# A shifted-mean LN1 apply, another order of the first loads, and a new step table in a fused adaLN, linear-attention and gated-MLP kernel

## The chip, the cores and the metric

The kernel runs on one core of a Trainium2 chip. The metric is the device time of one execution in microseconds (us); lower is better. The time before is the median of three runs, 279.08 us (278.98 to 279.73). One further execution was profiled; the views of the profile all come from that one.

A core has five engines that run at the same time, each with an in-order queue of its own: PE (TensorE, matmuls; its weight loads are listed as PEld), DVE (VectorE), ACT (ScalarE), POOL (GpSimd) and SP (SyncE, which here only issues transfers). An instruction waits at the head of its queue until the semaphores that it needs have come, and everything behind it on that engine waits with it.

## The reference, cut to what matters

The input is x, 2048 rows of 448 numbers in bf16, and a condition vector c. `mod = silu(c) @ w_mod` gives six vectors of 448: shift, scale and gate for each of two blocks.

```
h = layernorm(x) * (1 + ca) + sa
x = x + ga * A(h)          # attention with softmax feature maps, 16 heads of 28
h = layernorm(x) * (1 + cb) + sb
x = x + gb * B(h)          # gated MLP with a mixing matrix over the rows
```

A takes q, k and v from `h @ wqkv`, maps q and k per head by `w_phi`, and forms the features `concat(softmax(p), softmax(-p))`; `kv` and `z` are sums over all 2048 rows, and the output is `(phi_q kv) / (phi_q z)`, times `wo`. B computes `z = gelu(h @ w_in)`, splits it into z1 and z2 (896 columns each), normalises z2, mixes it over the rows with a 2048x2048 matrix `w_sp`, and returns `(z1 * (w_sp z2 + b_sp)) @ w_out`. Layernorm is `(x - mean) / sqrt(var + eps)` over the 448 columns.

## The kernel before, in words

The rows are cut into 16 tiles of 128. The program is one fixed sequence of some 800 steps. A table, `ORDER`, names them in order; a loop at the end of `fast_path` reads the words one after the other and calls the function of each. A word is `name:arguments/engine@slot`: `l1a:4/G` is step `l1a` for tile 4 on POOL, V is DVE, S is ACT, Y is SP; `@A2` names the PSUM slot. There are five slots, A0, A1 and A2 of two banks and B0 and B1 of one; a step that takes a slot waits until the step that reads out the slot's last user is done. Since the queues are in order, the table fixes each engine's sequence. Nothing is reordered later.

The stages and their steps, in the words of the table:

- **Loads** (`ld:`): x in six pieces (x0 to x5), wq, wk, wv, w_phi, pieces of w_mod (wsa and wca for the first block, wsb and wcb for the second, wmga and wmgb for the gates), wo, w_in in two halves (win0, win1), wout and bsp. They go out on SP's queue (Y) or ACT's (S). `W:t,u` loads a piece of `w_sp` through a transposing transfer, 32 in all, on SP's queue. The transfers of both queues share eight completion semaphores in rotation, so that a transfer is issued only once the eighth transfer before it has landed.
- **Condition**: `ct` and `ce` make silu(c); `csA`, `ccA` (and `csB`, `ccB` for the second block) multiply it with w_mod on PE; `esA`, `ecA`, `esB`, `ecB` read the result out.
- **Weights of the first block**: `FT` transposes wq or wk (raw) on PE, `ET` copies it out, `PF` multiplies it with w_phi, `EP` copies that out into `f_Wq` or `f_Wk`; `SH` adds the shift as a row, `SC` scales the rows by (1 + ca). `SHw` and `SCw` do the same for w_in in the second block.
- **LN1**: `l1s` takes mean and variance of a tile on DVE (L803, L804); `l1e` adds eps (L807); `l1r` raises to the power -0.5 on POOL (L810); `l1a` writes the normalised tile into `f_xpad` (L813), in one instruction of two operations: subtract the mean, multiply with the reciprocal root. Tiles 0 to 3 are then turned on PE (`X`, `XE`), tiles 4 to 15 in pairs by a transposing transfer on SP's queue (`T1:a,b`), into `f_hT`.
- **Features of k and sums**: for each tile `kM` (PE), `kE` and `kF` (two exponentials on ACT), `kS` (sums, DVE), `kR` (reciprocal, DVE), `kP` (multiply, DVE or POOL); `vM` (PE) and `vC` (ACT); `kA` adds the tile's share of kv on PE into slot A0. After the last one `KV` (DVE) reads the sums out. `qM` (PE, eight steps, two per four tiles) with `qE` and `qF` (ACT) make the features of q.
- **Attention output**: `nM` (PE), `nX` (ACT), `nC`, `nS`, `nT` (DVE), `nA`, then a transposing transfer `T2`, `wM` or `wN` (PE; `wN` adds x by an identity matmul), `wR` and `wQ` (sums for LN2).
- **LN2 and w_in**: `l2R`, `l2r`, `l2a` (L973: one instruction that adds the negated mean and multiplies), a transfer `T3`, then `zM` with `zG`, `zQ`, `zR`, `zW`, `zN` for z2 and `yM` with `yG` for z1.
- **Mixing and output**: 28 `gM` of 16 matmuls each, `gG`, then `oM`, `oE` and the store `oD`.

`du` runs matmuls on zeros, which only keep PE running; `tbl` runs one small exponential on ACT. `guard` and `read` take a flag that chooses a general path, which is not taken here.

The lines that the change touches, besides the table, are L807 and L813.

Of the kernel before, what the change touches and what calls it, by code (L numbers as in the profile page):

```python
# [486 lines left out]
l1a:3/G l1s:5 X:2@B1 SCk:3/S PFq:3@A2 SCk:0/V PFq:2@A1 X:3@A0 EPq:3/S XE:2/V PFq:0@B0 SCk:1/S PFq:1@A2 EPq:2/V vM:2@B1 SCk:2/S l1s:6 EPq:1/S kM:0@A1
vC:2 l1s:7 EPq:0/S kM:1@A2 XE:3/V kE:0 l1e:4,8/G kM:2@B0 l1r:4,8 kF:0 l1s:8 kF:1 vM:3@B1 kS:0 kE:2 l1a:6/G SHq@A1 kE:1 l1s:9 kF:2 l1a:5/G kM:3@A2 vC:3
kS:1 SCq:2/S gr:0@B0 SCq:0/S SCq:1/V csB@B1 W:0,7 kF:3 SCq:3/V kR:1 qM:0@A1 ge:0 l1a:4/V esB kE:3 kR:0 l1a:7/V T1:4,6 kP:0/V kP:1/G ccB@B0 kS:2 qF:0
kA:0@A0 T1:6,8 qM:1@A2 kS:3 qE:0 kR:2 ecB kR:3 kP:2/G kA:1@A0 l1s:10 ld:wmgb/Y qF:1 vM:4@B0 l1s:11 W:0,5 qE:1 kM:4@B1 kP:3/G l1s:12 kA:2@A0 vC:4  # L490
l1s:13 kM:5@A2 kE:4 l1s:14 kF:4 kM:6@B0 l1e:8,12/G kE:5 l1r:8,12 kS:4 kA:3@A0 kF:5 kM:7@B1 kE:6 l1a:9/G kS:5 kF:6 qM:2@A2 kE:7 l1a:11/G kR:4 kF:7 kR:5
l1a:8/G kS:6 qM:3@A1 T1:8,10 qE:2 kP:4/V kP:5/G l1s:15 qF:2 kA:4@A0 W:0,6 kR:6 l1a:10/V qE:3 vM:5@B0 vM:6@B1 qF:3 kP:6/V T1:10,12 l1e:12,16/V kM:8@A2
kS:7 l1r:12,16 vC:5 kM:9@A1 ld:wo/S ld:bsp/Y kR:7 kE:8 l1a:12/G l1a:14/V kA:5@A0 kF:8 vM:7@B0 l1a:13/G vC:6 kP:7/V kE:9 vM:8@A2 kF:9 l1a:15/G T1:12,14
kA:6@A0 vC:7 kS:8 kM:10@B1 vC:8 T1:14,16 kA:7@A0 kS:9 wos:2/G kE:10 kM:11@B0 kF:10 kR:8 wos:0/G vM:9@A2 kR:9 kE:11 kS:10 kF:11 vM:10@B1 vC:9 kP:8/V
vM:11@B0 vC:10 kP:9/V kA:8@A0 kR:10 vC:11 kM:12@B1 kS:11 kA:9@A0 kE:12 kP:10/V kM:13@B0 kF:12 kR:11 kA:10@A0 kP:11/G kS:12 kF:13 kM:14@B1 kE:13
vM:12@A2 kR:12 kE:14 kS:13 kP:12/G kF:14 kA:11@A0 vC:12 kM:15@B0 kS:14 ld:win0/S vM:13@B1 kF:15 kR:13 kR:14 kE:15 kA:12@A0 kP:13/V W:0,0 vC:13
vM:14@A2 kP:14/V kA:13@A0 kS:15 vC:14 vM:15@B0 kR:15 kA:14@A0 vC:15 kP:15/G qM:4@A2 ld:win1/S tbl wos:3/G SHw:0@B0 qE:4 kA:15@A0 qM:5@A1 KV:1 qF:4
KV:0 SCw:0,0/S SHw:1@B1 wos:1/V qE:5 nM:0@A2 SCw:1,0/G SCw:2,0/V qF:5 nM:1@A0 SHw:3@B0 nX:1 nX:0 SCw:0,1/S nC:1 nM:2@A1 nC:0 nS:0 SCw:0,3/S SHw:2@B1
# [28 lines left out]
def fast_path(tc, A_x, A_wqkv, A_w_phi, A_wo, B_w_in, B_w_sp, B_b_sp, B_w_out, c, w_mod, out, flag):  # L527
# [277 lines left out]

    def l1e(a, b, eng):
        eng.tensor_scalar(out=rs1[:, a:b], in0=mv1[:, a:b, 1], scalar1=LN_EPS, scalar2=None, op0=ALU.add)  # L807
# [335 lines left out]
```

## Time and profile before

| | us |
|---|---|
| median of three runs | 279.08 |
| lowest, highest | 278.98, 279.73 |
| the profiled execution's own time | 278.33 |
| its span (first to last instruction) | 276.4 |
| PE busy | 258.0 |
| DVE busy | 158.0 |
| ACT busy | 115.1 |
| POOL busy | 79.9 |

The profiled execution took 1.93 us more than its span, and 0.75 us less than the median. In the views, a row of a timeline or of the chain of waits begins with a start and a duration in us; a group's row gives a count, the busy time and the mean duration in ns; a row of the view by windows gives the stretch, its length, the busy time of each engine with its number of instructions, the clock that PE was granted (1.00 is full), the busy share of the DMA engines, and GB/s.

### The profile page before, as it was taken

The numbers are of one execution on the slowest core, as the hardware profiler recorded it, in microseconds if no ns is written. First come the engines' busy times: TensorE is split into PE (matmuls) and PEld (weight loads), VectorE is DVE, ScalarE is ACT, GpSimd is POOL, SyncE is SP. The second block draws the span as 40 slices with busy tenths as digits, with TensorE's granted clock in tenths as the row PEclk, the third lists the DMA queues.
The fourth block names the chain that finished last, engine by engine and source line by source line (L and its number), as shares of the span: only waits on it lengthen the run. The fifth ranks groups of instructions, "written<-read, shape, count | busy, mean of one in ns | idle before, by whom it ended". The sixth has DMA issues, their size and how long they took to land.

```text
span 276.4 us, 4119 instructions
## 1 busy us (share of the span) xinstructions
PE 258.0 (93%) x1522; PEld 133.4 (48%) x1533; DVE 158.0 (57%) x371; ACT 115.1 (42%) x242; POOL 79.9 (29%) x86
## 2 busy tenths in 40 slices
...
GB/s 187 285 289 61 87 88 162 168 35 192 43 76 107 161 147 115 51 193 103 137 185 162 21 0 0 2 0 17 50 92 166 48 2 53 16 0 33 2 35 76
DMA packets 68654, 25.21 MB, mean 91 GB/s; under 512 B 58129, under 2 KB 68498, under 8 KB 68626
## 3 DMA queue, kind: packets, MB, share of 16 engines
...
## 4 chain that ended last, share of the span: by engine, by line
PE 76%; POOL 6%; DVE 6%; issue 4%; ACT 3%; DMA 3%; POOLq 0%; DVEq 0%; ACTq 0%
PE g_ps L1025 35%; PE z_ps L984 9%; PE z_ps L1012 9%; PE o_ps L1037 7%; POOL f_xpad L813 4%; PE v_ps L844 3%; PE k_ps L836 3%; PE x_ps L944 3%; PE q_ps L884 3%; PE kvacc L867 2%; DMA f_hT<-f_xpad 1%; DVE f_t L928 1%; DMA f_x<-in_A_x_dram 1%; ACT f_win L757 1%; ACT f_Eq L889 1%
## 5 line engine op out<-in xcount | busy, mean ns | idle before, releaser
L1025 PEld LDWEIGHTS <-f_z2n 128*128 128x128 bf16 x448 | 43.7, 98 | 52.4
L1030 DVE TENSOR_TENSOR f_gb<-g_ps,f_bsp 128x512 f32<-128x512 f32 x28 | 19.3, 690 | 57.6 <-PE g_ps L1025 57.5
L1025 PE MATMUL g_ps<-f_Eq,f_z2n 128*128 128x512 bf16 x218 | 49.2, 379 | 0.3
L1015 ACT ACTIVATE f_z1T<-z_ps 128x512 bf16<-128x512 f32 x28 | 15.7, 598 | 53.8 <-PE z_ps L1012 53.7
L984 PE MATMUL z_ps<-f_win,f_hT 112*128 112x448 bf16 (+1 forms) x128 | 26.0, 352 | 0.1
L1012 PE MATMUL z_ps<-f_hT,f_win 113*128 113x512 bf16 (+1 forms) x112 | 25.8, 379 | 0.0
L1025 PE MATMUL g_ps<-f_hT,f_z2n 128*128 128x512 bf16 x110 | 24.6, 379 | 0.1
L1025 PE MATMUL g_ps<-f_wsp,f_z2n 128*128 128x512 bf16 x109 | 24.0, 379 | 0.2
L813 POOL TENSOR_SCALAR f_xpad<-f_x,f_mv,f_rs 128x448 bf16<-128x448 bf16 x12 | 22.8, 1909 | 0.5
L1037 PE MATMUL o_ps<-f_wout,f_z1T 128*128 128x448 bf16 x112 | 22.3, 353 | 0.0
L850 DVE TENSOR_REDUCE f_ksum<-f_E 128x32 f32<-128x896 bf16 x16 | 16.9, 1067 | 7.0 <-ACT f_E L839 7.0
L1031 DVE TENSOR_TENSOR f_z1T<-f_gb,f_z1T 128x512 bf16<-128x512 f32 x28 | 19.5, 696 | 1.2
L839 ACT ACTIVATE f_E<-k_ps 128x448 bf16<-128x448 f32 x32 | 15.6, 551 | 6.8 <-issue 4.2
L984 PEld LDWEIGHTS <-f_hT 112*128 112x128 bf16 (+1 forms) x128 | 12.4, 97 | 12.2 <-issue 0.3
L836 PE MATMUL k_ps<-f_Wk,f_hT 113*128 113x448 bf16 (+1 forms) x64 | 14.3, 355 | 3.8 <-DMA f_hT<-f_xpad 3.8
L889 ACT ACTIVATE f_Eq<-q_ps 112x1024 bf16<-112x1024 f32 x16 | 15.6, 1024 | 4.7 <-PE q_ps L884 4.7
L1012 PEld LDWEIGHTS <-f_win 113*128 113x128 bf16 (+1 forms) x112 | 10.8, 97 | 12.6
L928 DVE TENSOR_TENSOR f_t<-num,f_w 128x896 bf16<-128x896 f32 x16 | 16.8, 1083 | 0.2
L1037 PEld LDWEIGHTS <-f_z1T 128*128 128x128 bf16 x112 | 10.9, 98 | 10.6
L988 ACT ACTIVATE f_z2g<-z_ps 128x896 bf16<-128x896 f32 x16 | 14.7, 916 | 2.0 <-PE z_ps L984 1.9
L844 PE MATMUL v_ps<-f_wv,f_hT 113*128 113x448 bf16 (+1 forms) x64 | 15.3, 379 | 0.0
L857 POOL TENSOR_TENSOR f_phik<-f_E,f_kr 128x896 bf16<-128x896 bf16 x7 | 11.8, 1687 | 12.3 <-DVE f_kr L854 8.7
...
## 6 DMA issues: line engine op xcount, KB each, us to landing
...
f_wmg<-in_w_mod_dram SPq DMA_DIRECT2D x2, 392.0 KB, 6.6
...
```

The lines of the kernel that those rows point to most:

```text
L813: eng.tensor_scalar(out=xpad[:, i % NX, :, 0:CB], in0=x_sb[:, i, :].rearrange("p (k e) -> p k e", k=KC), scalar1=mv1[:, i, 0:1], scalar2=r ...
L836: nc.tensor.matmul(t[:, 0, 0:D], lhsT=hT[0:KR[m], i, m, :], rhs=Wk[0:KR[m], m, :], start=(m == 0), stop=(m == KC - 1))
L844: nc.tensor.matmul(t[:, 0, 0:D], lhsT=hT[0:KR[m], i, m, :], rhs=wv[0:KR[m], m, :], start=(m == 0), stop=(m == KC - 1))
L850: nc.vector.tensor_reduce(out=ksum[:, i], in_=Er[i % NR][:].rearrange("p s (c f h) -> p (s c) h f", c=4, h=HP), axis=AX.X, op=ALU.add)
L889: nc.scalar.activation(out=Eq[st // 2][0:CB, 2 * c2:2 * c2 + 2, s, (st % 2) * 512:(st % 2 + 1) * 512], in_=ps["q" + str(n)][0:CB, :, :], f ...
L928: nc.vector.tensor_tensor(out=tr[i % 2][:], in0=numv(i)[:, :, :, 0:DH], in1=wr[i // 2 % 2][:, i % 2].unsqueeze(3).to_broadcast([P, 2, H, D ...
L984: nc.tensor.matmul(t[:, hf, 0:D], lhsT=hT[0:KR[m], i, m, :], rhs=win_s[0:KR[m], m, FH + hf * D:FH + (hf + 1) * D], start=(m == 0), stop=(m ...
L1012: nc.tensor.matmul(t[:, 0, :], lhsT=win_s[0:KR[m], m, fc * P:(fc + 1) * P], rhs=hT[0:KR[m], 4 * st:4 * st + 4, m, :], start=(m == 0), stop ...
L1025: nc.tensor.matmul(g[:, 0, :], lhsT=later["z2n"][:, s_, fc * P:(fc + 1) * P], rhs=wspT[t][:, s_, :], start=(s_ == 0), stop=(s_ == NT - 1))
L1030: nc.vector.tensor_tensor(out=gb[:], in0=ps["G%d_%d" % (t, fc)][:, 0, :], in1=bsp[:, t * TCHF:(t + 1) * TCHF], op=ALU.add)
L1031: nc.vector.tensor_tensor(out=z, in0=gb[:], in1=z, op=ALU.mult)
L1037: nc.tensor.matmul(ps["o" + str(t)][:, 0, 0:D], lhsT=later["z1T"][:, fc, t * P:(t + 1) * P], rhs=wout_s[:, fc, :], start=(fc == 0), stop=( ...
```

## The change

Three things change. `l1e` gets a second instruction, which writes the negated mean of the same tiles into a new array `f_nm`, and `l1a` adds that instead of subtracting the mean; the multiplication stays. The first loads go out in another order: c is first on ACT's queue with wq behind it, and x0 is first on SP's, followed by w_phi and wk. The table is new as a whole: the same steps (but for the `du` words, which now run 19 matmuls instead of 27), many in other places, on other slots and some on other engines. On other engines are, counted over the table: `SCw` 10 on ACT (before 7, with 2 on POOL and 1 on DVE), `SCv` 4 on ACT (3), `ET` all four on ACT (2 of 4), `l2a` 8 on POOL (4 of 16), `wR` 11 on ACT (9), `wQ` 10 on ACT (13), `zN` 3 on POOL (6), `nA` 6 on POOL (4), `XE` 3 on ACT (1), and one step each of `EP`, `zQ` and two of `wos`; 11 of the 16 tiles of the attention output go by `wN` (9). `kP` and `l1a` keep their split between DVE and POOL.

```
 ORDER = """
-ld:x0/S ld:wsa/Y ld:x1/Y ld:c/Y m1/V m2b/G du:15@A2 ld:wv/Y ld:wca/Y m3 l1s:0 ld:wk/Y m2a/G ld:x2/Y l1e:0,1/V ld:phi/Y m4 ld:wq/Y l1s:1 ct@B0 ld:x3/Y
...
+ld:c/S ld:x0/Y ld:wq/S ld:phi/Y tbl ld:wk/Y m3 du:1@A2 m1/V ld:x1/Y m2b/G ct@B0 ld:wsa/Y du:8@A2 ce:1 l1s:0 ld:x2/Y m4 ld:wca/Y ce:2 ld:wv/Y m2a/G
+FTq:0@B1 ld:x3/Y ce:3 bd/V W:0,1 FTq:1@A2 ETq:0/S l1e:0,1/G du:3@A1 ce:4 ETq:1/S ld:x4/Y FTk:1@B0 scb l1s:1 PFq:2@B1 FTk:0@A2 ETk:1/S l1r:0,1 EPq:2/V
...
     rs1 = aph.tile([P, NT], F32, name="f_rs1")
+    nm1 = aph.tile([P, NT], F32, name="f_nm1")
...
     def l1e(a, b, eng):
         eng.tensor_scalar(out=rs1[:, a:b], in0=mv1[:, a:b, 1], scalar1=LN_EPS, scalar2=None, op0=ALU.add)
+        eng.tensor_scalar(out=nm1[:, a:b], in0=mv1[:, a:b, 0], scalar1=-1.0, scalar2=None, op0=ALU.mult)
...
     def l1a(i, eng):
-        eng.tensor_scalar(out=xpad[:, i % NX, :, 0:CB], in0=x_sb[:, i, :].rearrange("p (k e) -> p k e", k=KC), scalar1=mv1[:, i, 0:1], scalar2=rs1[:, i:i + 1],
-                          op0=ALU.subtract, op1=ALU.mult)
+        eng.tensor_scalar(out=xpad[:, i % NX, :, 0:CB], in0=x_sb[:, i, :].rearrange("p (k e) -> p k e", k=KC), scalar1=nm1[:, i:i + 1], scalar2=rs1[:, i:i + 1],
+                          op0=ALU.add, op1=ALU.mult)
```

Three places show how the table moves instructions. In the changed kernel a line number is one or two higher than before.

**ACT, from the condition to the first features.** Before, in the order of the queue (`f_hT` is `XE`, `f_wTk` and `f_wTq` are `ET`, `f_Wk<-pf_ps` and `f_Wq<-pf_ps` are `EP`, an `f_ca` operand marks `SC`, `f_vaug` is `vC`, `f_E` is `kE` or `kF`):

```order
L717 ACTIVATE f_e<-ct_ps 112x4
L784 COPY f_hT<-xt_ps 128x512
L757 ACTIVATE f_wv<-f_wv,f_ca_139 112x448 x2
L757 ACTIVATE f_wv<-sh_ps,f_ca_139 113x448
L634 DMA f_wm_122<-in_w_mod_dram 112x4x464
L784 COPY f_wTk<-tps 112x896
L847 CAST f_vaug<-v_ps 128x16x28 x2
L784 CAST f_Wk<-pf_ps 112x448 x3
L784 COPY f_wTq<-tps 112x896
```

In the changed kernel:

```order
L718 ACTIVATE f_e<-ct_ps 112x4
L785 COPY f_wTq<-tps 112x896 x2
L785 COPY f_wTk<-tps 112x896 x2
L785 CAST f_Wq<-pf_ps 112x448 x2
L785 CAST f_Wk<-pf_ps 112x448
L785 COPY f_hT<-xt_ps 128x512
L785 CAST f_Wk<-pf_ps 112x448 x2
L644 DMA f_x<-in_A_x_dram 128x4x448
L785 COPY f_hT<-xt_ps 128x512
L758 ACTIVATE f_Wq<-f_Wq,f_ca_139 112x448 x2
L758 ACTIVATE f_Wk<-f_Wk,f_ca_139 112x448
L758 ACTIVATE f_wv<-f_wv,f_ca_139 112x448
```

The four copies of the transposed weights now stand first, ahead of any `XE`, and the `SC` steps come after the `EP` steps.

**POOL, the LN1 tiles 4 to 11 among the `kP` steps** (`f_xpad` is `l1a`, `f_phik` is `kP`, `f_rs<-f_rs` is `l1r`). Before:

```order
L810 TENSOR_TENSOR f_rs_145<-f_rs_145,f_mhalf 128x4
L813 TENSOR_SCALAR f_xpad<-f_x,f_mv_144,f_rs_145 128x4x112 x2
L857 TENSOR_TENSOR f_phik<-f_E_127,f_kr_133 128x896
L857 TENSOR_TENSOR f_phik<-f_E_128,f_kr_132 128x896
L857 TENSOR_TENSOR f_phik<-f_E_129,f_kr_133 128x896
L807 TENSOR_SCALAR f_rs_145<-f_mv_144 128x4
L810 TENSOR_TENSOR f_rs_145<-f_rs_145,f_mhalf 128x4
L813 TENSOR_SCALAR f_xpad<-f_x,f_mv_144,f_rs_145 128x4x112 x3
```

In the changed kernel:

```order
L812 TENSOR_TENSOR f_rs_145<-f_rs_145,f_mhalf 128x4
L815 TENSOR_SCALAR f_xpad<-f_x,f_nm_146,f_rs_145 128x4x112 x2
L812 TENSOR_TENSOR f_rs_145<-f_rs_145,f_mhalf 128x4
L815 TENSOR_SCALAR f_xpad<-f_x,f_nm_146,f_rs_145 128x4x112 x3
L859 TENSOR_TENSOR f_phik<-f_E_127,f_kr_133 128x896
L859 TENSOR_TENSOR f_phik<-f_E_128,f_kr_132 128x896
L859 TENSOR_TENSOR f_phik<-f_E_129,f_kr_133 128x896
L815 TENSOR_SCALAR f_xpad<-f_x,f_nm_146,f_rs_145 128x4x112
```

Tiles 11, 10 and 8 are now applied ahead of the first three `kP` on POOL; only tile 9 is left behind them.

**SP, the loads around the last `T1` transfers** (`f_hT<-f_xpad` is `T1`, `f_wm` is wcb here, `f_wsp` is `W`). Before, wcb stood on ACT's queue, as the DMA row above. In the changed kernel:

```order
L628 DMA f_win<-in_B_w_in_dram 112x4x896
L820 DMA_TRANSPOSE f_hT<-f_xpad 128x8x128 x2
L659 DMA f_bsp<-in_B_b_sp_dram 128x2048
L628 DMA f_win<-in_B_w_in_dram 112x4x896
L1022 DMA_TRANSPOSE f_wsp_84<-in_B_w_sp_dram 128x8x128
L635 DMA f_wm_122<-in_w_mod_dram 112x4x464
```

wcb now stands on SP's queue behind the last two `T1` transfers, bsp, one half of w_in and a piece of `w_sp`; `ccB`, which reads it, stands on PE right ahead of the first `nM`.

More of the change, by code (lines that the diff above doesn't have):

```diff
@@ L487 @@
[L487 to L498, printed above, removed]
@@ L523 @@
[L523 removed]
+ld:c/S ld:x0/Y ld:wq/S ld:phi/Y tbl ld:wk/Y m3 du:1@A2 m1/V ld:x1/Y m2b/G ct@B0 ld:wsa/Y du:8@A2 ce:1 l1s:0 ld:x2/Y m4 ld:wca/Y ce:2 ld:wv/Y m2a/G
+FTq:0@B1 ld:x3/Y ce:3 bd/V W:0,1 FTq:1@A2 ETq:0/S l1e:0,1/G du:3@A1 ce:4 ETq:1/S ld:x4/Y FTk:1@B0 scb l1s:1 PFq:2@B1 FTk:0@A2 ETk:1/S l1r:0,1 EPq:2/V
+PFq:3@A1 ETk:0/S l1e:1,2/V PFq:1@B0 l1a:0/G PFq:0@B1 csA@A0 EPq:1/V EPq:3/S l1r:1,2 PFk:1@A2 EPq:0/S esA X:0@B0 l1s:2 PFk:0@A1 EPk:1/S l1a:1/G
```

66 lines of the change are left out of this document (38 added, 28 removed).

## The prediction

> **What bounds the kernel now.** I began with the busy times of the page, then asked what PE waited for longest, then took PE's stretches by windows.
>
> ```profile
> span 276.4 us, 4119 instructions
> PE 258.0 (93%) x1522; PEld 133.4 (48%) x1533; DVE 158.0 (57%) x371; ACT 115.1 (42%) x242; POOL 79.9 (29%) x86
> ```
>
> ```profile
> PE k_ps L836 <- DMA f_hT<-f_xpad: 3.8, 1, 3.8
> ```
>
> ```profile
> 8.00:12.70 4.70, 3.95 (x33) 2.73 (x34) 0.92 (x3) 1.72 (x4) 3.65 (x4) 0.50 1.14 273
> 27.20:43.60 16.40, 16.20 (x137) 9.00 (x135) 16.15 (x37) 13.70 (x22) 12.34 (x10) 1.00 0.43 74
> 43.60:47.40 3.80, 0.03 (x1) 0.00 (x1) 1.74 (x4) 0.57 (x2) 3.70 (x3) 1.00 0.97 224
> 47.40:52.50 5.10, 5.10 (x24) 2.72 (x25) 2.65 (x4) 2.82 (x6) 5.10 (x4) 0.67 0.80 214
> 77.10:79.20 2.10, 0.05 (x1) 0.05 (x2) 2.03 (x7) 0.22 (x2) 0.03 (x1) 1.00 0.31 69
> 79.20:84.30 5.10, 4.94 (x34) 2.98 (x34) 4.92 (x10) 2.11 (x8) 3.71 (x2) 0.67 0.50 107
> 98.00:148.60 50.60, 50.60 (x277) 25.40 (x277) 33.38 (x115) 44.15 (x105) 17.98 (x21) 1.00 0.73 132
> 148.60:269.40 120.80, 120.22 (x564) 55.81 (x573) 49.54 (x79) 4.94 (x9) 2.37 (x2) 1.00 0.18 37
> ```
>
> PE bounds the kernel. From 98 us to the last matmul it has no gap worth a name, at the full clock. What can be gained lies ahead of 98 us: in the start (clock 0.50 until 12.7), in the 3.8 us without a matmul at 43.6, in 2.1 us at 77.1, and in the slow clock (0.67) that follows each of these gaps. The chain of waits shows where the large gap comes from:
>
> ```profile
> 39.78 3.71 POOL f_xpad L813 x2
> 43.51 3.85 DMA f_hT<-f_xpad
> 47.40 1.87 PE k_ps L836 x8
> 52.68 0.42 PE kvacc L867 x8
> 53.10 0.76 PE k_ps L836 x4
> 66.33 1.74 PE q_ps L884 x8
> 28.12 0.39 PE cf_ps L734 x16
> ```
>
> LN1 tiles on POOL one after the other, then the transfer, then k. The 24 matmuls of the window from 47.4 (8 for k, 8 for kv, 8 for v) took 5.1 us or a little more; four k matmuls take 0.76 in the later row (v has the same shape) and eight of kv 0.42, so 3.46 at the full clock. This one wait cost 3.8 + 1.7 = 5.5 us.
>
> **The LN1 apply.** The same tile is written by two lines:
>
> ```profile
> L813 POOL TENSOR_SCALAR f_xpad<-f_x,f_mv,f_rs x12: 1852/1859/2433, 6.8 to 50.5; 128x448 bf16<-128x448 bf16 x12
> L973 POOL TENSOR_SCALAR f_xpad<-f_x,f_m,f_v x4: 708/711/727, 88.0 to 108.4; 128x448 bf16<-128x448 bf16 x4
> L807 POOL TENSOR_SCALAR f_rs<-f_mv 128x4 f32<-128x4 f32 x2 | 0.5, 236 | 1.3 <-DVE f_mv L804 1.3
> ```
>
> L973 adds a negated mean where L813 subtracts a mean; shape, types, source and destination agree. So I price `l1a` on POOL at 0.71 us: 12 x (1.86 - 0.71) = 13.8 us less POOL work. The new second instruction of `l1e` costs 0.24 us, six times, of which each LN1 chain pays one. POOL itself is 29% busy, so this is worth only what waits behind it, the transfers `T1` and `kP`. The gap at 43.6 goes: tile 9, the one left behind three `kP`, is now 0.71 long, and a pair's transfer comes earlier than its `kM`. In its place the pace of the whole stage decides.
>
> **The first features: ACT sets the start.** With wq and wk first, their folding no longer waits for the condition. Loads land at some 272 GB/s:
>
> ```profile
> 4.00:8.00 4.00, 2.35 (x30) 1.56 (x28) 2.48 (x10) 0.17 (x1) 2.24 (x5) 0.98 1.12 272
> 2.07 0.34 SPq L627 DMA_DIRECT2D f_wv<-in_A_wqkv_dram  x1
> f_wv<-in_A_wqkv_dram SPq DMA_DIRECT2D x1, 392.0 KB, 5.2
> 12.72 1.70 PE L780 MATMUL tps<-f_ident,f_wk_raw 112*112 112x112 bf16 x16
> ```
>
> Before, wv landed at 7.3 us, with 1.02 MB issued up to it; ahead of wq there is now as much as 0.9 MB (c, x0, w_phi, and wk in step with it), so wq lands near 6.7 us. Eight cold transposes (half of 1.70) make it 7.5. From there ACT's queue has, ahead of the first `qM`:
>
> ```profile
> L784 ACT COPY f_wTk<-tps x1: 905/905/905, 14.5 to 14.5; 112x896 bf16<-112x896 bf16 x1
> L784 ACT CAST f_Wk<-pf_ps x3: 532/537/547, 16.6 to 17.6; 112x448 bf16<-112x448 f32 x3
> L784 ACT COPY f_hT<-xt_ps x1: 585/585/585, 9.4 to 9.4; 128x512 bf16<-128x512 bf16 x1
> L757 ACT ACTIVATE f_Wk<-f_Wk,f_ca x3: 656/667/670, 19.2 to 21.0; 112x448 bf16<-112x448 bf16 x3
> ```
>
> Four `ET` of 0.905, five `EP` of 0.54, three `XE` of 0.585, four `SC` of 0.67 and a transfer's issue (0.34) are 11.1 us, so `qM:0` starts near 18.6 us. Until then PE has about 7 us of work (folds, shifts, X): it is covered by ACT, and so are the eight zero matmuls that are gone. PE's work from `qM:0` to the first `nM`, by the rows above: 32 x 0.76 for k and v, 16 x 0.42 for kv, 6 x 1.75 for q, 0.76 for the gate (four matmuls of k's length) and 2 x 0.39 for the second condition: 43.1 us. Nothing less than 18.6 + 43.1 = **61.7 us** is possible for the first `nM`. Before it was:
>
> ```profile
> 71.57 1.00 PE L912 MATMUL num<-f_KVbd,f_Eq 112*128 112x120 bf16 x16
> 92.68 1.68 PE L984 MATMUL z_ps<-f_win,f_hT 113*128 113x448 bf16 x8
> L850 DVE TENSOR_REDUCE f_ksum<-f_E 128x32 f32<-128x896 bf16 x16 | 16.9, 1067 | 7.0 <-ACT f_E L839 7.0
> L854 DVE RECIPROCAL f_kr<-f_ksum 128x32 bf16<-128x32 f32 x16 | 5.1, 337 | 1.2 <-POOL f_phik L857 1.1
> L857 DVE TENSOR_TENSOR f_phik<-f_E,f_kr 128x896 bf16<-128x896 bf16 x9 | 5.4, 624 | 0.0
> L803 DVE BATCH_NORM_STATS2 f_st<-f_x 128x6 f32<-128x448 bf16 x16 | 9.7, 605 | 2.3 <-DMA f_x<-in_A_x_dram 2.3
> ```
>
> The bound won't be reached. In these 43 us DVE has 16.9 + 5.1 + 5.4 us of `kS`, `kR` and `kP`, most of the 9.7 and of the small ops of `l1s`, some 37 us in all; ACT has about as much in 32 exponentials, 16 `vC` and 12 feature maps of q. Three engines at 85% or more, tied by five PSUM slots and four buffers, lose something. I allow 0.8 us for slots at the start (`kM:0` takes B0 from `vM:0`, whose `vC` stands behind two `SCk` and a `qF` on ACT), 1.7 for a cold clock once, as after 47.4, and 1.5 for waits between the three: 4.0, first `nM` at 65.7, **5.9 us** earlier. The bounds of this term are 9.9 (no allowance) and about 2 (twice the allowance).
>
> **From the first `nM` to the first `zM`** it was 92.68 - 71.57 = 21.1 us, of which PE idled or ran slow for 5.6. Two more `SHw` (1.5 us) now fall in it. By the queues each `nM` still waits for `nT`, so they fill holes; but all of `SCw` is on ACT between the `nX`, and three `wos` precede the first `nC` on DVE. I take +0.3, between -1 and +2. A wait as at 77.1 stays.
>
> The Trainium skill (TensorE: Matmul & The Clock Gate, Part 1) says that the clock is halved after an idle window of about 3.4 us. By that, a 2 us hole is followed by no slow stretch, and the two or three short holes here and in the stage before would leave the sum up to 1.7 us lower. The row for 79.2 to 84.3, 0.67 after a hole of 2.1 us, speaks against it, so I keep the cold clock.
>
> **The rest.** Two more `wN` add two identity matmuls of the length of an x tile: +0.4. The `W` pieces for the last quarter go into `f_hT` after the last `yM`:
>
> ```profile
> 202.52 11.65 SPq L1020 DMA_TRANSPOSE f_hT<-in_B_w_sp_dram  x8
> f_hT<-in_B_w_sp_dram SPq DMA_TRANSPOSE x8, 4.2
> 183.14 3.97 PE o_ps L1037 x21
> 235.02 10.74 PE g_ps L1025 x49
> ```
>
> They need 11.65 + 4.2 = 15.9 us, with two stores in between some 16.5. Behind the last `yM` PE has now eight `oM` of 1.32 (3.97 for three) and two `gM` of 3.5 (16 of 49 in 10.74): 17.6 us. That hides it by 1 us; each us beyond would be paid in full. wcb must be there before `ccB`: behind the last `T1`, issued near 46 us, stand bsp (0.5 MB), win0 (0.8), a piece of `w_sp` (0.26) and wcb (0.4), with wout (0.8) beside them; 2.75 MB at 214 GB/s land near 60 us, ahead of 65, at 150 GB/s near 65. Nothing is added for either. Between 98 and 148.6 ACT changes little: two `wR` more, three `wQ` and one `zQ` less.
>
> Sum: -5.9 + 0.3 + 0.4 = -5.2 on the span, 271.2; with the 1.93 us around it, 273.1. The median stood 0.75 above the profiled run; I add half, 0.4: **273.5 us**.
>
> **The rivals.**
>
> *The three engines keep step* (0.17). If there is neither a cold clock nor waiting, the first `nM` comes at 62 to 63: 269.5 to 270.5 us. For it: 52.5 to 66.1 ran without a loss. Against: there DVE was 77% and ACT 69% busy.
>
> ```profile
> 52.50:66.10 13.60, 13.60 (x124) 8.74 (x123) 10.54 (x17) 9.38 (x20) 5.21 (x4) 1.00 0.43 102
> ```
>
> *The swap doesn't shorten `l1a`* (0.06). L813 and L973 run at different times, and place might set the duration. Five `l1a` more at 1.15 us put the transfer of tiles 8 and 9 5.8 us later; by my count along POOL's and PE's queues it has a reserve of about 1.5 ahead of `kM:8`, so PE waits 4.3, and with 1.7 of cold clock 6 us come back: 279. Against: the twelve lie between 1.85 and 2.43 us over 44 us, beside an idle DVE and a full one. The Trainium skill (GPSIMD Engine Reference, 3.1) counts cycles per element by port and number of operations, and by it a subtract costs what an add does; the trace's 1.86 against 0.71 disagrees, and decides.
>
> *The feature stage stalls again and again* (0.09; slower). The place is `kM` and `kA` between 23 and 65 us: PE waits for an `kE` or `kP` that is late on ACT or DVE, goes cold, and so on. One such wait, by the windows from 77.1, costs 2.1 us and about 1.7 of slow clock, 3.8. One more than allowed gives 277.3; with the second the gain is gone: 281. For it: DVE was 16.15 of 16.4 us busy from 27.2 to 43.6. Against: in that very stretch PE lost only 0.2.
>
> The forecast itself, 271 to 277, has 0.68.
>
> **How the numbers follow.** About 0.3% (0.8 us) is what a measurement of this kernel can tell from no change. Faster: the forecast, the first rival and a little of the second, 0.85; same: most of the second and the edge of the third, 0.06; slower: 0.09. The range reaches from the bound without allowance, 269.5, to one stall more, 277.5; some 0.16 is outside.
>
> **What would show it.** Right: `l1a` on POOL at 0.7 us; ACT without a gap from 7.5 to beyond 18 us; first `qM` near 18.6, first `nM` at 64 to 67, first `zM` 21 us later; no wait of k for `f_hT` over 1 us; full PE from there. Wrong: a POOL `l1a` of 1.8 us; a first `qM` after 21; PE holes of 2 us or more before the last `kA`; PE waiting for wcb ahead of the first `nM`, or for `f_hT` in the mixing.

## The result, and the profile after

The changed kernel took 270.56 us (median of four runs, 270.05 to 271.23) against 279.03 for the kernel before on the same chip: a ratio of 0.969, with a 95% interval of 0.966 to 0.972, so 8.5 us or 3.1% less. The forecast was 273.5, with a range of 269.5 to 277.5. The direction and the range held; the time lies at the lower end of the range, next to the number of the first rival (269.5 to 270.5) and 2.9 us under the forecast. In what follows, executions more than 1.5% above the fastest of their kernel on a chip are left out of the medians; the kernel before then has 279.03, 278.15, 278.59 and 278.86 us on the four chips used, so times of different chips can be compared to some 1 us. The profiled execution took 270.05 us, 268.3 of them span. From the page of the changed kernel:

```profile
span 268.3 us, 4100 instructions
PE 252.3 (94%) x1516; PEld 130.5 (49%) x1527; DVE 156.5 (58%) x372; ACT 118.9 (44%) x245; POOL 62.7 (23%) x88
```

PE is busy 5.7 us less: it runs less at half clock, and eight zero matmuls are gone. POOL is busy 17 us less. The instructions on the tile `f_xpad`, for the LN1 apply (minimum, median and maximum in ns, then first and last start):

```profile
L815 POOL TENSOR_SCALAR f_xpad<-f_x,f_nm,f_rs x12: 717/718/732, 7.3 to 41.3; 128x448 bf16<-128x448 bf16 x12
L815 DVE TENSOR_SCALAR f_xpad<-f_x,f_nm,f_rs x4: 366/390/1755, 15.4 to 39.7; 128x448 bf16<-128x448 bf16 x4
```

The apply takes 0.72 us on POOL where it took 1.86. What PE waits for, in place of the 3.8 us for `f_hT`:

```profile
PE num L914 <- DVE f_t L930: 2.9, 3, 1.6
PE tps L781 <- DMA f_wq_raw<-in_A_wqkv_dram: 2.2, 1, 2.2
```

PE's order of time shows the steps of the prediction: start, duration, what, and in brackets the idle time ahead and who ended it.

```profile
6.53 1.74 PE L781 MATMUL tps<-f_ident,f_wq_raw 112*112 112x112 bf16 x16 [2.15 <-DMA f_wq_raw<-in_A_wqkv_dram]
17.46 1.89 PE L886 MATMUL q_ps<-f_hT,f_Wq 113*128 113x512 bf16 x8 [0.41 <-ACT f_hT L785]
61.56 1.42 PE L914 MATMUL num<-f_KVbd,f_Eq 112*128 112x120 bf16 x24 [0.31 <-DVE f_cb L739]
65.81 0.58 PE L914 MATMUL num<-f_KVbd,f_Eq 112*128 112x120 bf16 x8 [0.43 <-DVE f_t L930]
69.17 0.58 PE L914 MATMUL num<-f_KVbd,f_Eq 112*128 112x120 bf16 x8 [1.61 <-DVE f_t L930]
72.98 0.59 PE L914 MATMUL num<-f_KVbd,f_Eq 112*128 112x120 bf16 x8 [0.90 <-DVE f_t L930]
82.65 1.69 PE L986 MATMUL z_ps<-f_win,f_hT 113*128 113x448 bf16 x8 [0.41 <-DMA f_hT<-f_xpad]
```

And its stretches by windows (length; busy time of PE, PEld, DVE, ACT and POOL with the count of instructions; PE's granted clock; DMA share; GB/s):

```profile
17.46:61.56 44.10, 43.52 (x341) 24.77 (x340) 38.17 (x76) 36.59 (x66) 23.02 (x21) 1.00 0.79 175
67.50:69.17 1.67, 0.06 (x2) 0.00 (x0) 1.53 (x4) 1.67 (x5) 0.00 (x0) 1.00 0.35 79
69.17:72.10 2.93, 2.90 (x26) 1.71 (x25) 2.72 (x9) 2.93 (x7) 1.03 (x1) 1.00 0.30 69
262.40:268.30 5.90, 0.00 (x0) 0.00 (x0) 0.02 (x1) 0.00 (x0) 0.00 (x0) 0.77 0.19 59
```

From the first `qM` to the first `nM` PE is busy 43.52 of 44.10 us, all at full clock. The hole at 77.1 of the kernel before is still there, at 67.5, but it is 1.61 us long where it was 2.1, and the clock behind it stays at 1.00 where it fell to 0.67. After the last VectorE add, at 262.4, comes a tail of 5.9 us, in which only stores and the end of the program are left; before it was 4.7 (the last add ended at 271.69 of 276.4).

### The profile page after: what moved, and what is told of

Read it like the earlier page. It is cut to its first block, busy times and chain, and to the rows that moved or that the text cites. A ratio compares the mean times of both kernels' runs of the same rounds, so it can differ in the third digit from the quotient of the medians.

```text
span 268.3 us, 4100 instructions
## 1 busy us (share of the span) xinstructions
PE 252.3 (94%) x1516; PEld 130.5 (49%) x1527; DVE 156.5 (58%) x372; ACT 118.9 (44%) x245; POOL 62.7 (23%) x88
## 4 chain that ended last, share of the span: by engine, by line
PE 71%; DVE 12%; ACT 7%; DMA 3%; issue 2%; POOL 1%; SPq 0%; ACTq 0%; DVEq 0%
PE g_ps L1027 36%; PE z_ps L986 9%; PE z_ps L1014 9%; PE o_ps L1039 7%; DVE f_ksum L852 5%; PE x_ps L946 3%; DMA f_wq_raw<-in_A_wqkv_dram 2%; DVE f_phik L859 2%; DMA f_hT<-f_xpad 1%; ACT f_win L758 1%; ACT f_Eq L891 1%; PE num L914 1%; PE q_ps L886 1%; DVE f_kr L856 1%; PE tps L781 1%
## 5 line engine op out<-in xcount | busy, mean ns | idle before, releaser
L1027 PE MATMUL g_ps<-f_Eq,f_z2n 128*128 128x512 bf16 x219 | 48.6, 379 | 0.3
L859 POOL TENSOR_TENSOR f_phik<-f_E,f_kr 128x896 bf16<-128x896 bf16 x7 | 12.7, 1823 | 12.7 <-PE k_ps L838 10.8
L886 PE MATMUL q_ps<-f_hT,f_Wq 113*128 113x512 bf16 (+1 forms) x64 | 15.2, 379 | 0.4 <-ACT f_hT L785 0.4
L1042 DVE TENSOR_TENSOR f_xpad<-o_ps,f_x 128x448 bf16<-128x448 f32 x16 | 9.1, 618 | 10.7 <-PE o_ps L1039 10.7
L946 PE MATMUL x_ps<-f_wo,f_oT 112*128 112x448 bf16 x64 | 14.7, 352 | 0.3 <-DMA f_oT<-f_opad 0.3
```

Of the source, the lines that this page charges most:

```text
L859: eng.tensor_tensor(out=pr[i % NR][:, 0:2 * D].rearrange("p (a f h) -> p a f h", a=8, h=HP), in0=Er[i % NR][:].rearrange("p s (c f h) -> p ...
L886: nc.tensor.matmul(t[:, u, :], lhsT=Wq[0:KR[m], m, cc * CB:cc * CB + P], rhs=hT[0:KR[m], 4 * st:4 * st + 4, m, :], start=(m == 0), stop=(m ...
L946: nc.tensor.matmul(t[:, 0, 0:D], lhsT=oT[0:CB, i % 4, cc, :], rhs=wo_s[0:CB, cc, :], start=(cc == 0 and not with_x), stop=(cc == KC - 1))
L1027: nc.tensor.matmul(g[:, 0, :], lhsT=later["z2n"][:, s_, fc * P:(fc + 1) * P], rhs=wspT[t][:, s_, :], start=(s_ == 0), stop=(s_ == NT - 1))
```

## The experiments

The theory: the gain has two sources, the short form of the LN1 apply and the early wq, and from the first `qM` on PE alone sets the pace, with VectorE next. Rivals: that only one of the two did it; that the order alone did it; that the places of c and x0 on their queues matter in themselves.

**The old form in the new order.** The apply subtracts the mean again, and `l1e` has lost its second instruction; order and loads are those of the changed kernel.

```diff
-        eng.tensor_scalar(out=nm1[:, a:b], in0=mv1[:, a:b, 0], scalar1=-1.0, scalar2=None, op0=ALU.mult)
...
-        ... scalar1=nm1[:, i:i + 1], scalar2=rs1[:, i:i + 1], op0=ALU.add, op1=ALU.mult)
+        ... scalar1=mv1[:, i, 0:1], scalar2=rs1[:, i:i + 1], op0=ALU.subtract, op1=ALU.mult)
```

> The changed kernel with the LN1 apply back in its old form (subtract of the mean, then times the reciprocal deviation; no negated mean), its order and loads kept. Theory (the form is what makes POOL's apply short, and the new order needs it): the 12 POOL applies take 1.85 us again instead of 0.72, POOL falls some 5 us behind by tile 8, PE waits for the transposes of f_hT between about 27 and 45 us, first num matmul at 64 to 67 us instead of 61.6, time +3 to +6 us on the changed kernel (273.5 to 276.5). Rival (the form is a side matter, POOL has room for the slow form in the new order): applies 1.85 us but the time within 1 us of the changed kernel's 270.6. Second rival (the duration comes from the order, not from the form): applies 0.72 us with subtract too.

277.71 us: 7.1 more than the changed kernel, and nearly all of the gain gone (ratio to before 0.995, interval 0.991 to 0.999). The profiled execution, at 279.61, is the slowest of ten, so its waits are on the high side. The apply on POOL, PE's waits, one hole in the order of time, and the windows of this kernel:

```profile
L813 POOL TENSOR_SCALAR f_xpad<-f_x,f_mv,f_rs x12: 1858/1861/1957, 7.0 to 47.4; 128x448 bf16<-128x448 bf16 x12
PE k_ps L836 <- DMA f_hT<-f_xpad: 2.8, 2, 1.9
PE kvacc L867 <- POOL f_phik L857: 2.2, 4, 1.0
PE v_ps L844 <- DMA f_hT<-f_xpad: 0.7, 1, 0.7
53.09 0.93 PE L836 MATMUL k_ps<-f_Wk,f_hT 113*128 113x448 bf16 x4 [1.87 <-DMA f_hT<-f_xpad]
17.50:69.60 52.10, 46.10 (x343) 25.23 (x341) 38.47 (x76) 37.38 (x66) 31.94 (x20) 0.97 0.71 149
53.09:57.80 4.71, 4.71 (x22) 2.41 (x23) 2.36 (x4) 1.61 (x4) 0.00 (x0) 0.64 1.09 256
```

The first `qM` comes at 17.55 as in the changed kernel, and the first `nM` at 69.6, 8.0 us later. POOL falls behind with the applies and with the `kP` queued behind them: 2.8 + 0.7 us of waits for `f_hT`, 2.2 for `f_phik`, and a clock of 0.64 behind the 1.87 us hole. So it is the form that makes the apply short, in the new order as well, and the new order needs it. The loss was larger than forecast, since not only the transfers but also `kP` stood behind the slow apply on POOL.

**The new form in the old order.** The converse: the kernel before with only these lines of the diff.

> The kernel before, order and loads kept, with only the new form of the LN1 apply (add of the negated mean). Theory: POOL's applies take 0.72 us, the 3.8 us hole of PE at 43.6 us in front of the k matmuls is gone or below 1 us, with the clock at 0.67 behind it gone too; time -3.5 to -5.5 us on the 279.0 before (273.5 to 275.5). Rival (the hole had a second cause close behind, DVE or the transposes' queue): hole shrinks by half or less, time -2 us or less. If the form gives 4 to 5.5 here and 3 to 6 in the other run of this pair, the new order and loads alone give only the rest of the 8.5 us.

274.94 us, 3.2 under the 278.15 of the kernel before on this chip; ratio 0.982 (0.973 to 0.991). The four executions lie apart, and with them PE's mean granted clock: 272.42 us at 0.999, 273.44 at 0.988, 276.45 at 0.978, and the profiled one, 276.49 at 0.979, the slowest. In that one PE's longest wait, 3.8 us before, is 2.3, but it is another wait:

```profile
PE k_ps L838 <- DMA f_hT<-f_xpad: 2.3, 1, 2.3
42.12 1.69 PE L838 MATMUL k_ps<-f_Wk,f_hT 113*128 113x448 bf16 x8
48.41 1.68 PE L838 MATMUL k_ps<-f_Wk,f_hT 113*128 113x448 bf16 x4 [2.25 <-DMA f_hT<-f_xpad]
48.41:51.60 3.19, 3.19 (x15) 1.81 (x16) 0.41 (x1) 0.98 (x2) 0.52 (x1) 0.50 1.21 191
76.15:83.00 6.85, 6.85 (x38) 4.27 (x39) 5.15 (x10) 2.84 (x11) 3.54 (x2) 0.55 0.45 98
```

By the medians the gain is just short of the theory's (-3.5 to -5.5), by the ratio, about 5 us, within it. The hole that the theory was about, ahead of the k of tile 8, is gone: the k of tiles 8 and 9 runs at 42.12 without a wait, where it ran at 47.40. The 2.25 us stand two tiles on, ahead of tile 10. Its tile was applied by 41.2 us and its transfer issued at 41.73, but the chain of waits has that transfer at 6.63 us from issue to landing; the transfer of this pair took 2.9 us in the kernel before. The loads of wo and bsp, 0.9 MB issued at 41.56 and 43.03, run beside it; whether they slow it, no run tested. The new hole has a slow clock behind it too (0.50 for 3.2 us), and 0.55 for 6.9 us follows behind the later hole. The other gain lies ahead, where PE waits 0.4 us for single tiles of the apply (2.5 us in three waits before): the first `qM` starts at 26.3 us where it was 28.4. The swap of `l1a` alone is thus worth some 3 us by the medians and 5 by the ratio in the old order, with an interval of 2.5 to 7.5, and 7.1 in the new one.

**The new order with the old loads.** The first 13 loads are issued in the order and on the queues of the kernel before.

```diff
-ld:c/S ld:x0/Y ld:wq/S ld:phi/Y ... ld:wk/Y ... ld:x1/Y ... ld:wsa/Y ... ld:x2/Y ... ld:wca/Y ... ld:wv/Y ... ld:x3/Y ... ld:x4/Y ... ld:x5/S
+ld:x0/S ld:wsa/Y ld:x1/Y ld:c/Y ... ld:wv/Y ... ld:wca/Y ... ld:wk/Y ... ld:x2/Y ... ld:phi/Y ... ld:wq/Y ... ld:x3/Y ... ld:x5/Y ... ld:x4/Y
```

> The changed kernel, with its first 13 loads issued in the order and on the queues of the kernel before (x0 alone on ACT's queue; on SP's queue wsa, x1, c, wv, wca, wk, x2, phi, wq, x3, x5, x4), all else kept. Theory (the landing of wq starts ACT's gapless 10 us of work ahead of the first q matmul): wq lands at 12.5 to 13.5 us instead of 6.5, first q matmul at 23 to 24.5 us instead of 17.5, first num matmul about 67 to 68, time +5 to +7 us on the changed kernel (275.5 to 277.5). Rival (DVE and POOL, not the landing, set the pace of the feature stage, and later work catches up): +2 us or less.

277.06 us, 6.5 over the changed kernel (ratio to before 0.998, 0.993 to 1.003). Three rows of its order of time:

```profile
13.24 1.74 PE L785 MATMUL tps<-f_ident,f_wq_raw 112*112 112x112 bf16 x16 [5.71 <-DMA f_wq_raw<-in_A_wqkv_dram]
24.17 1.89 PE L890 MATMUL q_ps<-f_hT,f_Wq 113*128 113x512 bf16 x8 [0.41 <-ACT f_hT L789]
67.87 1.42 PE L918 MATMUL num<-f_KVbd,f_Eq 112*128 112x120 bf16 x24 [0.32 <-DVE f_cb L743]
```

Folding starts 6.7 us later, the first `qM` 6.7 later, the first `nM` 6.3 later: nearly the whole delay of wq reaches the end. (The run moves thirteen loads at once; that it is wq among them goes by the times of the folding.) From `qM` to `nM` it is 43.7 us, next to the 43.1 of PE work that the prediction counted. Form and loads, taken back one at a time, cost 7.1 and 6.5 us, together more than the 8.5 that both gave: the order is made for both, and nearly all of the gain is lost if either is missing. Without the new loads the new table gains nothing: with the new form and the old loads it took 277.06 us, the old table on the same chip 274.94. No run has the new loads with the old table, so what they would give there is open.

**c and x0 exchanged between their queues.**

```diff
-ld:c/S ld:x0/Y ld:wq/S
+ld:x0/S ld:c/Y ld:wq/S
```

> The changed kernel with only c and x0 exchanged between the queues: x0 first on ACT's queue ahead of wq, c first on SP's queue. Theory (wq's landing matters, where c stands does not): 112 KB of x0 ahead of wq on its queue move wq's landing from 6.5 to 7 to 7.5 us, the first q matmul by as much, time +0.3 to +1.0 us. Rival (the place of c and x0 on their queues carries a good part of the gain): +2 us or more. Second rival: no change, within 0.3%, because all queues share the same 16 engines.

269.44 us (268.86 to 270.35), not slower, as the second rival had it. The folding of wq starts at 6.11 us. In the executions with c ahead of wq on ACT's queue it started between 5.64 and 6.59, so 112 KB more ahead of it on that queue cannot be seen. On another chip the changed kernel itself took 269.97. Which queue has c and which x0 does not count. What the two kernels share is that wq is issued at 1.1 to 1.3 us, where the kernel before issues it at 5.2; with the run before this one that makes its early issue the likely part that counts. The theory's +0.3 to +1.0 is a miss.

**Three `kP` from POOL to VectorE.**

```diff
-kP:2/G ... kP:3/G ... kP:4/G
+kP:2/V ... kP:3/V ... kP:4/V
```

> The changed kernel with three of the seven kP products that POOL does (tiles 2, 3 and 4, between about 30 and 42 us) moved to VectorE, each 0.60 us there instead of 1.8 on POOL. Theory (TensorE, VectorE and POOL are planned level from 24 to 54 us; VectorE was busy 5.65 and 6.00 of 6 us in the two stretches concerned, so it has some 0.4 us left): the 1.8 us shift VectorE's queue by about 1.4 us, first num matmul at 62.5 to 63.5 us instead of 61.6, time +0.8 to +1.8 us. Rival (TensorE alone sets the pace and the rings of buffers take up the shift): first num matmul within 0.4 us, time within 0.5 us.

272.08 us, 1.5 over the changed kernel, and 1.2 to 1.8 over the kernels of the next three experiments on this chip, which leave `kP` where it was (270.90, 270.27 and, in one execution, 270.36). Its PE has one new hole, and the first `nM` comes 45.2 us after the first `qM` (at 17.13), where it was 43.7 to 44.1:

```profile
40.61 0.59 PE L873 MATMUL kvacc<-f_vaug,f_phik 128*128 128x116 bf16 x8 [0.89 <-DVE f_phik L863]
62.34 1.42 PE L918 MATMUL num<-f_KVbd,f_Eq 112*128 112x120 bf16 x24 [0.31 <-DVE f_cb L743]
```

1.8 us more on VectorE cost 1.1 to 1.5 on the way: VectorE has at most 0.7 us to spare there. TensorE and VectorE are nearly level in this stage, and the changed kernel gets through it without a wait worth naming.

**A longer hole at 67.5.** One VectorE add of 128x448 whose result nobody uses, ahead of `nT:2`; then three of them.

```diff
+    def xd():
+        nc.vector.tensor_tensor(out=junk2[:, 0:D], in0=x_sb[:, 15, :], in1=x_sb[:, 15, :], op=ALU.add)
...
-... nT:2 ...
+... xd nT:2 ...
```

> The changed kernel with one additional VectorE add of 128x448 bf16 (0.39 us, its result unused) just ahead of the num product of tile 2, so that TensorE's 1.61 us hole at 67.5 us becomes about 2.0 us. Theory (what the granted clock does after a hole goes by the hole's length: 1.00 was granted after 1.61 us, 0.50 for 3 us and more after 1.87, 2.05 and 2.25 us): granted clock 0.50 for 3 to 5 us behind the hole; time +0.4 for the addition and +0.5 to +2 for the slow clock. Rival (the clock goes by something else, the load before the hole or the place in the program): clock 1.00 behind the hole, time +0.2 to +0.5 us.

> The changed kernel with three additional VectorE adds of 128x448 bf16 ahead of the num product of tile 2 (results unused), so that TensorE's hole there becomes 2.2 to 2.8 us. Theory (the clock behind a hole goes by its length, with the border between the 1.72 us that left it at 1.00 and the 1.87 us that halved it): granted clock 0.50 for 3 us or more behind the hole, and time +1.5 to +3.5 us on the changed kernel. Rival (place or load decide): clock 1.00, time +0.5 to +1.2 us, the additional work alone.

With one addition the hole became 1.72 us and not 2.0, since VectorE had a short gap there and its operations overlap somewhat, and the clock stayed at 1.00; the time, 270.90, says nothing on the question, so the run was too weak. With three the time was 271.65, 1.7 over the changed kernel on the same chip (269.97):

```profile
69.16 0.96 PE L918 MATMUL num<-f_KVbd,f_Eq 112*128 112x120 bf16 x8 [2.57 <-DVE f_t L934]
69.16:75.60 6.44, 6.44 (x36) 3.96 (x36) 4.76 (x11) 3.17 (x9) 2.06 (x2) 0.52 0.58 122
75.60:84.05 8.45, 8.45 (x56) 4.50 (x55) 6.85 (x25) 7.48 (x18) 2.82 (x4) 1.00 0.76 143
```

After 2.57 us the clock is 0.52 for 6.4 us, and eight num matmuls take 0.96 us instead of 0.58. The first z comes 23.5 us after the first `nM` (60.59 to 84.05) where the changed kernel needed 20.6 on this chip: 2.9 more, 1.0 of it in the longer hole. At the end 1.7 are left, as a wait of 1.37 us for `f_oT` at 84 us, which the changed kernel has on this chip, is no longer there. So at the same place and under the same load a longer hole brings the slow clock. How much of it varies between executions: the four had a mean clock of 0.981 to 0.993 and took 270.26 to 272.34 us; the fourteen executions of the changed kernel and of the run with one addition, whose profiled holes are 1.61 and 1.72 us, had 0.990 to 0.997.

**wo scaled early.** The gate's row, its copy and the scaling of wo move ahead of the `KV` products, where VectorE waited 3.87 us.

```diff
-kR:15 qM:4@A2 ... qM:5@A1 qF:4 kA:15@A0 qE:5 gr:0@B0 KV:1 ... ge:0 esB ecB
-nM:0@A1 wos:2/V nM:1@A2 wos:3/V nX:0 W:0,7 nM:2@A0 wos:0/V ...
+kR:15 gr:0@B1 ge:0 qM:4@A2 ... kA:15@A0 qM:5@A1 qF:4 qE:5 wos:2/V wos:3/V wos:0/V wos:1/G KV:1 ... esB ecB
+nM:0@A0 nM:1@A2 nX:0 W:0,7 nM:2@A1 ...
```

> The changed kernel with the gate row gr:0 computed ahead of the fifth q matmul group, its copy ge:0 behind it, the scaling of wo (three pieces on VectorE, 1.83 us together, one on POOL) ahead of the KV products, where VectorE waited 3.87 us, the last kvacc group ahead of the sixth q group, and the two larger PSUM slots exchanged behind. Theory (VectorE is the engine that sets the pace from 61.7 to 73 us, and the 1.83 us of wo stand in its queue ahead of the first nC): first nC at about 62.4 instead of 63.5 us, TensorE's holes of 0.43, 1.61 and 0.90 us shrink by 0.9 to 1.5 us in all, first z matmul at 81.2 to 81.8 instead of 82.65, time -0.8 to -1.5 us on the changed kernel. Rival (ACT's scaling of w_in in front of the copies of Sx sets the pace): holes as long as before, time within 0.4 us.

270.27 us (269.68 to 271.15). VectorE did start `nC` earlier, at 62.14 instead of 63.48, and the first z came 20.6 us after the first `nM`, 0.5 under the 21.1 of the first profile of the changed kernel; but the second profile of the changed kernel has 20.6 as well. The largest hole stays, and a wait stands behind z, as it does in the second profile of the changed kernel (1.37 us):

```profile
68.37 0.58 PE L918 MATMUL num<-f_KVbd,f_Eq 112*128 112x120 bf16 x8 [1.72 <-DVE f_t L934]
83.67 0.93 PE L950 MATMUL x_ps<-f_wo,f_oT 112*128 112x448 bf16 x4 [0.66 <-DMA f_oT<-f_opad]
```

No gain in time and a miss in mechanism: the holes are nearly as long as before, as the rival had it (2.7 us in two waits for `nT`, 2.9 in three in the changed kernel). VectorE is earlier from `nC` on, and so is the first `nM` (60.70 us), so the waits between the two keep their length. The rival's reason, ACT, the trace bears out in part: VectorE now waits 1.10 and 0.46 us for ACT's copies of Sx, which it did not in the changed kernel.

**Forms of `tensor_scalar` on POOL.** Fourteen additional operations late in the program, where POOL is idle, on 128x448 bf16, two of each form.

```diff
+    def pf():
+        o, i = junk2[:, 0:D], x_sb[:, 15, :]
+        a, b = m2[:, 0:1], v2[:, 0:1]
+        F = [(ALU.add, ALU.mult), (ALU.subtract, ALU.mult), (ALU.mult, ALU.add), (ALU.mult, None), (ALU.add, None), (ALU.subtract, None), (ALU.mult, ALU.mult)]
...
+                    nc.gpsimd.tensor_scalar(out=o, in0=i, scalar1=a, scalar2=None, op0=p)
...
+                    nc.gpsimd.tensor_scalar(out=o, in0=i, scalar1=a, scalar2=b, op0=p, op1=q)
```

> The changed kernel with 14 additional POOL operations of the LN1 apply's kind (tensor_scalar, 128x448 bf16 to bf16, one number per partition; results unused) late in the program, where POOL is idle: two each of add then mult, subtract then mult, mult then add, mult alone, add alone, subtract alone, mult then mult. Theory (POOL has a fast way for some forms and a slow one for subtract): add then mult 0.72 us, subtract then mult 1.85, subtract alone 1 us or more; what mult alone takes decides whether only subtract is slow. Rival (the LN1 apply's slowness lay in its operand, the mean read out of the pair of mean and variance): all two-operation forms 0.72 us.

All two-operation forms and all single ones among the fourteen, in two rows of the view by tile:

```profile
L1075 POOL TENSOR_SCALAR f_junk<-f_x,f_m,f_v x8: 708/714/1878, 140.1 to 157.3; 128x448 bf16<-128x448 bf16 x8
L1073 POOL TENSOR_SCALAR f_junk<-f_x,f_m x6: 1400/1409/1677, 147.2 to 154.8; 128x448 bf16<-128x448 bf16 x6
```

Singled out by windows: add then mult 0.71 us, subtract then mult 1.86 and 1.88, mult then add 0.71, mult then mult 0.71; mult alone and add alone 1.40 to 1.42, subtract alone 1.41 and 1.68. All fourteen read the same kind of operands. So it is the operation and not its operand that makes the old apply slow, and a single operation takes twice as long as two. The run was taken once, and serves for these durations only.

**The last store on SP's queue, and the changed kernel again.**

```diff
-oD:15/S
+oD:15/Y
```

> The changed kernel once more, so that the next two stand beside it on the same chip: 270 to 271 us. Its last output store, on ACT's queue, took 0.34 us to issue in the first profile and 1.3 to 2.0 in five of the experiments built on it; theory: that comes and goes from run to run, rival: it is the same in every run of one kernel and was 0.34 here.

> The changed kernel with only the last output store, oD:15, moved from ACT's queue to SP's. Theory (the issue of the last of ACT's twelve stores stalls in many runs for 1 to 1.7 us): -0.5 to -1.3 us on the changed kernel on the same chip. Rival (the stall moves with the store, or the tail is set by the store's landing): within 0.3 us.

On one chip the changed kernel took 269.97 us (269.23 to 270.40) and with the store moved 269.43 (268.79 to 269.75), 0.5 less, with ranges that overlap: the lower edge of the forecast, and near its rival (within 0.3). The issues on ACT's queue, from the changed kernel's first and second profile (minimum, median, maximum):

```profile
L1045 ACTq DMA_DIRECT2D out_dram<-f_xpad x11: 337/338/375, 216.0 to 262.4; - x11
```

```profile
L1045 ACTq DMA_DIRECT2D out_dram<-f_xpad x11: 338/339/1338, 214.9 to 261.4; - x11
```

So the long issue comes and goes with one and the same program. It is a small part of the tail: over the ten profiles with this store on ACT's queue and the new order, the tail is 5.9 us in the three with an issue of 0.34 to 0.38 us, and 6.3 to 7.2 in the seven with 1.34 to 2.03; with the store on SP's queue it is still 6.0.

**All of it together.** The early wo, `oD:15` on SP's queue, `nM:3` ahead of the third `SHw`, and two of ACT's `SCw` on POOL behind `nA:0`, as multiply then add zero.

```diff
+        elif eng is nc.gpsimd:
+            eng.tensor_scalar(out=out_, in0=in_, scalar1=sc, scalar2=0.0, op0=ALU.mult, op1=ALU.add)
...
-SHw:2@B0 ... SCw:3,0/S nA:0/G nM:3@A1 SHw:3@B1 nX:3 SCw:1,0/S ... oD:15/S
+nM:3@A0 SHw:2@B0 ... nA:0/G SCw:3,0/G SCw:1,0/G SHw:3@B1 nX:3 ... oD:15/Y
```

> The early scaling of wo as run before, and with it: oD:15 on SP's queue, the num group of tile 3 ahead of the third sh group of w_in, and two of ACT's scalings of w_in on POOL behind its first nA, as multiply then add zero (0.71 us for 448 columns where multiply alone took 1.41). Theory (after the first num group VectorE sets the pace and waits 0.46 us for a copy of Sx that stands behind ACT's scaling): first z matmul 0.3 to 0.6 us earlier after the first num group than with the early wo alone (20.6 us there, 21.1 in the changed kernel), time 1.0 to 2.5 us under the changed kernel on the same chip, 267.5 to 269.5. Rival (the transposes of oT and hT behind it set z's start): no earlier z, time -0.5 to -1.0 us from the store and the early wo.

267.98 us (267.80 to 268.60): 2.0 under the changed kernel on the same chip (0.7%, every run below every one of that), ratio to the kernel before 0.961 (0.958 to 0.965). Where the 2 us come from is not what was forecast:

```profile
80.71 1.69 PE L992 MATMUL z_ps<-f_win,f_hT 113*128 113x448 bf16 x8
83.86 0.93 PE L952 MATMUL x_ps<-f_wo,f_oT 112*128 112x448 bf16 x4 [1.45 <-DMA f_oT<-f_opad]
259.01 2.22 DVE L1048 TENSOR_TENSOR f_xpad<-o_ps,f_x 128x448 bf16<-128x448 f32 x4 [2.36 <-PE o_ps L1045]
```

The first z comes 20.6 us after the first `nM` (60.08), as in the changed kernel on this chip, then PE waits for `f_oT` (1.45 us, 1.37 there), and the last VectorE add ends at 261.23 against 261.36 there. PE waits less for `nT` (2.4 us, 2.9 there), but z is no earlier, as the rival had it. In the profiled runs the difference lies behind the last add: a tail of 4.4 us (261.23 to 265.6) against 6.3 (261.36 to 267.7). Of these 1.9 us 0.6 come back outside the span: 2.38 us around it in this execution, 1.76 there.

## Why the prediction was right, and where its numbers were off

By its own steps:

| step | predicted | measured |
|---|---|---|
| `l1a` on POOL | 0.71 us | 0.72 |
| wq landed | near 6.7 us | 6.5 |
| first `qM` | 18.6 | 17.46 |
| first `qM` to first `nM` | 43.1 + 4.0 | 43.1 + 1.0 |
| first `nM` | 65.7 | 61.56 |
| first `nM` to first `zM` | 21.1 + 0.3 | 21.1 |
| first `zM` to the end | 183.7 + 0.4 | 183.7 + 1.9 |
| span | 271.2 | 268.3 |

**Right in mechanism.** The form of the apply is what shortens it (0.72 in one form, 1.86 in the other, in both orders and in a run of the forms alone), it removes the wait for `f_hT`, and wq's landing carries through ACT's queue to the first `nM` nearly one for one. PE's work from `qM` to `nM` was counted right: 43.1 against 43.52 busy. The rival that the swap does not shorten `l1a` is out, and its price was near: 279 forecast, 277.7 measured with the slow form, though in seven waits and not in one ahead of tile 8. Of the prediction's own signs of being right one did not come, the first `nM` at 64 to 67 us: it came at 61.56, and even under the 61.7 that the prediction gave as the least possible, since the first `qM` was 1.1 us earlier than counted.

**The largest error is the allowance of 4.0 us** ahead of the first `nM`: 0.8 for slots, 1.7 for a cold clock, 1.5 for waits between the engines. It measured 1.0 (44.10 less 43.1), and 0.6 in the second profile of the changed kernel (43.7). The argument was that three engines at 85% or more lose something. They hardly did: the order kept TensorE full although VectorE had 38.17 and ACT 36.59 us of work in the 44.10, and only 1.8 us more on VectorE opened a hole. The first rival, engines that keep step, had 0.17 and is what happened. That its time nearly came out as well is luck: its first `nM`, 62 to 63 us, was forecast some 1 us later than it came, and the end took 1.5 us more than counted. Without a hole above 0.4 us there was nothing to cool the clock either, so the 1.7 fell away with the rest.

**ACT's 11.1 us came out at 9.8.** It was a sum of single durations. ACT's order of time has two such copies in 1.71 us, though each of them lasts 0.908:

```profile
7.56 1.71 ACT L785 COPY f_wTq<-tps 112x896 bf16<-112x896 bf16 x2 [4.33 <-PE tps L781]
9.70 1.71 ACT L785 COPY f_wTk<-tps 112x896 bf16<-112x896 bf16 x2 [0.42 <-PE tps L781]
```

Operations that follow each other on ACT overlap by about 0.1 us here. The 16 durations sum to 10.9 us; the chain from 7.56 to 17.40 took 9.8, which is the sum less some 1.5 of overlap plus the one gap of 0.42. The transfer's issue, for which the prediction charged 0.34 us, ran beside a copy and cost nothing. That put the first `qM` at 17.46 instead of 18.6.

**The stretch to `zM` was right by two errors.** A wait as at 77.1 did stay, but at 1.61 us it no longer halved the clock, which had cost 1.7 us (a granted clock of 0.92 over these 21.1 us before, 1.00 now). Two more `SHw` (1.5 us) and 0.4 us more of idle time (2.9 before, 3.35 now, with new holes of 0.43 and 0.90) took the place of that. The Trainium skill (TensorE: Matmul & The Clock Gate, Part 1) names an idle window of about 3.4 us as what halves the clock; here 1.87 us was enough, so the row that the prediction quoted against it was right to count; what the row alone did not give was where the border lies.

**The end was worse than forecast by 1.5 us.** 1.2 of it is the tail (4.7 before, 5.9 after), which the prediction carried over unchanged; the rest lies between z and the last add (179.0 before, 179.8 after, with 0.4 forecast). The landing of wcb, and `f_hT` in the mixing, cost nothing, as forecast.

The errors add up to the miss on the span: 1.1 (first `qM`) + 3.0 (allowance) + 0.3 (to `zM`) - 1.5 (end) = 2.9.

**Still open.** Why the tail is 4.4 us in one kernel and 6.0 in another that ends with the same stores on the same queues (5.9 and 6.3 in the changed kernel). SP's waits at the end of the program differ along with it (the view of waits from 255 us on; total, times and longest), in the changed kernel and then in the combined one:

```profile
SPq L1112 <- SPq L1112: 3.6, 5, 2.4
SPq L1140 <- ACTq L1140: 1.5, 1, 1.5
```

```profile
SPq L1118 <- SPq L1118: 2.2, 4, 1.2
SPq L1146 <- PEq L1146: 0.6, 2, 0.5
```

The first row of each is at the branch around the general path, where SP waits for the stores to land; the second is the engines' meeting at the end of the program. In the trace the last store lands 2.85 us after the last add in the combined kernel and 2.80 in the second profile of the changed one, so between these two the 1.9 us lie behind the stores, in the program's end. Nothing that the combined kernel was meant to speed up stands there, and no run tested what sets it. How much of its 2.0 us would survive in another program is open with it.
